# Attention and a gated MLP on one core: new planner numbers, and one more head pair in split form

## The chip, the cores and the metric

The kernel runs on one core of a Trainium2 chip. The metric is the device time of one execution in microseconds (us). Three runs of the kernel before gave 720.61, 721.33 and 721.49 us; the median is 721.33. A further execution was taken with the hardware profiler: it lasted 721.01 us, with a span from the first to the last instruction of 719.0 us.

## The reference, cut to what matters

```python
batch, n_heads, seq, head_dim = (4, 12, 448, 64)
n_tokens, d_model, d_ff = (1792, 768, 1536)

scores = scale * np.matmul(q, k.transpose(0, 1, 3, 2))
scores = np.where(mask, -1000000000.0, scores)          # causal
scores = scores - np.max(scores, axis=-1, keepdims=True)
attn = np.exp(scores)
attn = attn / (np.sum(attn, axis=-1, keepdims=True) + 1e-09)
x = np.matmul(attn, v)                                   # heads side by side: 1792 x 768

g = x @ w_gate
silu = g * (1.0 / (1.0 + np.exp(-g)))
val = x @ w_val
out = silu * val @ w_out
```

## The kernel before, in words

The four batches are four chunks of 448 tokens. A chunk has 12 attention units (one head each; unit u belongs to chunk u // 12, and units go in six pairs), and then a gated MLP (called M for the first two products, MO for the last) of 36 weight tiles: 24 for gate and value, 12 for the output.

Attention of a unit, in the names that the profile shows: the scores S on TensorE (PE, line 434); the row maximum with the mask on VectorE (DVE, line 456); the exponential p with its sums on ScalarE (ACT, line 465); the reciprocal rec on DVE (lines 476 and 477); the scaling of p by rec, one instruction for each of four row blocks, on ACT (line 486), GpSimd (POOL, line 490) or DVE (line 494); ten transposes T on PE (line 515); the copy of T to ph out of PSUM on ACT (line 286) or DVE (line 289); the product O with V on PE; the copy of O into xs.

A pair is computed in one of two forms. In float32 form ("n" in the strings NS and NP) S and O are float32 matmuls of the raw q, k and v (tiles kraw, qraw, vraw; O on line 584). In split form ("s") every operand is first parted into a high and a low part in float32r (QS, KS, VS, ph with pl), and three products of the parts are added (S from KS and QS; O on lines 554 and 556). The parting is one copy (lines 286, 289, 292 for ACT, DVE, POOL) and one subtraction (lines 308 and 311 for DVE and POOL). `nat` reads a string with the index of the pair modulo its length, so 'ns' in batch 1 makes pairs 0, 2 and 4 float32. Batch 0 is all float32, batches 2 and 3 all split.

The MLP always uses the split form: three matmuls of 448 columns (lines 691 to 693) for each 128 x 128 block of weights, 2592 in all. For chunk 0 each of the 36 weight tiles is loaded as 64-bit words (wide), scaled in place, and unpacked on DVE in three steps (wraw: lines 664, 668 and 672), and then parted into whl (one copy, one subtraction); the parted tile is stored to DRAM and loaded from there in the later chunks. whl has five buffers. The input xs is parted into xh and xl, the gated product t into hh and hl.

The order of all instructions comes from a planner that runs when the kernel is built (class Planner, `run`): it walks through time, and for each engine takes the ready operation that starts first within DELTA of the earliest, the least due time first. Where an operation can run on several engines, `finish` gives it to the one on which its modelled end plus BIAS is least. The due times come from LEN (the length given to each of five stages), FRAC, FRAC0, SLOPE and SLOPE0 (attention), XD (parting of xs), WLEAD (weights) and BOOST (reading out of M). The instructions are then issued in the planned order, and each engine works through its own list in that order, waiting where an input is late.

Of the kernel before, what the change touches and what calls it, by code (L numbers as in the profile page):

```python
# [18 lines left out]
WID = [0, 64, 192, 320, 448]  # L19
CHUNKS = [[(0, 0, 448)], [(1, 0, 448)], [(2, 0, 448)], [(3, 0, 448)]]  # L20
NR = 8
SLOPE0 = 1.0
WLEAD = 1.2
XD = [-10.0, 3.0]
CS = 0.0
UW = 0
NS = ['n', 'ns', 's', 's']
NP = ['n', 'ns', 's', 's']
LEN = [46.6, 112.0, 258.9, 133.6, 58.1]
FRAC = 0.96  # L30
FRAC0 = 0.6
SLOPE = 1.0
BOOST = 6
DELTA = {'PE': 0, 'DVE': 0.1, 'ACT': 0.1, 'POOL': 0.4, 'SP': 0.0}
BIAS = {'DVE': 1.3, 'ACT': 0.8, 'POOL': 0.8}
PVLATE = 0
LAT = {"PE": 0.29, "DVE": 0.2, "ACT": 0.23, "POOL": 0.2, "SP": 0.1}
TURN = {'ms': 0.19, 'sm': 0.19, 'mt': 0.09, 'tm': 0.085, 'ts': 0.19, 'st': 0.19, 'mv': 0.15, 'vm': 0.15, 'tv': 0.15, 'vt': 0.15, 'sv': 0.15, 'vs': 0.15}
# [12 lines left out]
def nat(flags, b, h):  # L51
    f = flags[b]
    return f[(h // 2) % len(f)] == "n"
# [32 lines left out]
class Planner:  # L86
# [9 lines left out]
    def run(self, caps):  # L96
# [6 lines left out]
        def begin(o, e, t):  # L103
            if e == "POOL":
                return max(t, lock["DVE"])
            if e == "DVE" and o.port:
                return max(t, lock["POOL"])
            return t
# [14 lines left out]
        def ready(o, e):  # L123
            t = 0.0
            for d in o.deps:
                x = d.end if d in o.soft else d.end + d.extra + (LAT[d.eng] if d.eng != e else (0.0 if e == "PE" else 0.13))
                if x > t:
                    t = x
            for i, r in enumerate(o.alloc):
                h = slots(r.tag)[sum(x.tag == r.tag for x in o.alloc[:i])]  # L130
                if h is not None:
                    if h.left:
                        return None
                    if h.end > t:
                        t = h.end
            return t

        def finish(o, e, s):
            best = s + o.alts[e][0] + BIAS.get(e, 0.0)
            for f in o.alts:  # L140
                if f != e:
                    r = ready(o, f)
                    if r is not None and begin(o, f, max(r, free[f])) + o.alts[f][0] + BIAS.get(f, 0.0) + 1e-6 < best:
                        return False
            return True

        def choose(e):
# [9 lines left out]
            if not cand:  # L157
                return None
            lim = max(min(s for s, _ in cand), free[e]) + DELTA[e]
            if e == "PE" and kind == "t":  # L160
# [52 lines left out]
def raw(t):  # L213
    return t.bitcast(F32)
# [3 lines left out]
def kernel(  # L218
# [54 lines left out]
    def op(alts, due, deps=(), alloc=(), uses=(), extra=0.0):  # L273
        first = [heads[r.tag] for r in alloc if r.tag in heads]
        o = pl_.op(alts, due, list(deps) + first, alloc, uses, extra)
        o.soft = first
        o.port = bool(alts.pop("port", False))
        o.kb = alts.pop("kb", 0)
        o.kind = alts.pop("kind", "m")
        for r in alloc:  # L280
            heads[r.tag] = o
        return o

    def copies(kind, n, out, in_, scale=1.0, engines="ADP"):
        def act():
            nc.scalar.activation(out(), in_(), AF.Copy, scale=scale)  # L286

        def dve():
            nc.vector.tensor_scalar(out(), in_(), scale, None, ALU.mult)

        def gps():
            nc.gpsimd.tensor_scalar(out(), in_(), scale, 1.0, ALU.mult, ALU.mult)

        r = {}
        if "A" in engines:
            r["ACT"] = (cost("ACT", kind, n), act)
        if "D" in engines:
            r["DVE"] = (cost("DVE", "one" if kind == "sbuf" else "two", n), dve)
        if kind == "sbuf":
            r["port"] = True  # L300
        if "P" in engines and kind == "sbuf":
            r["POOL"] = (cost("POOL", "one", n), gps)
        return r
# [9 lines left out]

    start = [sum(LEN[:i]) for i in range(len(LEN))]
    class Unit:
        def __init__(self, c, b, h, qa, qb, col):
# [5 lines left out]
            self.n = qb - qa  # L322
            self.ns, self.np = nat(NS, b, h), nat(NP, b, h)

# [30 lines left out]
    def attention(u):  # L355
# [5 lines left out]
        frac = U.w0 / done_w[c]  # L361
        base = LEN[0] * FRAC0 * frac if c == 0 else start[c] + FRAC * LEN[c] * frac
        due = lambda stage: base + (SLOPE if c else SLOPE0) * stage
        if h % 2 == 0:
# [232 lines left out]
    def split_x(c, k):  # L597
        n = TC[c]
        rh, rl = Res(f"xh{k}"), Res(f"xl{k}")
        due = start[c + 1] + XD[1 if c else 0] + 0.2 * k  # L600
        rx = xs_res[c, k]
# [11 lines left out]
    def weights(i):  # L613
        c, g = seq[i]
        due = start[c + 1] + LEN[c + 1] * g / NW
        w = wt[i] = {}
# [6 lines left out]
        def split(ra, rw):  # L623
            def newh():
                newhl()
                return w["h"]
            h = op(copies("sbuf", WC, newh, lambda: w["raw"]), due - 6 * WLEAD, [ra], [rhl], [rw])
            l = op(binary(WC, lambda: w["l"], lambda: w["raw"], lambda: raw(w["h"])), due - 5 * WLEAD, [h], [], [rw, rhl])
            wops[i] = (h, l, rhl, rhl)
            return h, l  # L630

        def keep(dst, src, deps, use, kb):
            return op({"SP": (0.3, lambda: nc.sync.dma_start(dst, src())), "kb": kb}, due - 3 * WLEAD, deps, [], [use])

        if c and (g, "hl") in stored:
            def load():
                newhl()
                nc.sync.dma_start(raw(w["hl"]), scratch[g])
            ld = op({"SP": (0.3, load), "kb": 768}, due - 10 * WLEAD, [stored[g, "hl"]], [rhl])
            wops[i] = (ld, ld, rhl, rhl)  # L640
            return
        if c:
            rw = Res("wraw")

            def load():
                w["raw"] = buf([P, WC], F32, "wraw", "wraw", f"wraw{i}")
                nc.sync.dma_start(w["raw"], scratch1[g])
            ld = op({"SP": (0.3, load), "kb": 384}, due - 12 * WLEAD, [stored[g, "raw"]], [rw])
            h, l = split(ld, rw)
# [5 lines left out]
        def load():  # L655
            w["wide"] = buf([P, WC, 2], U32, "wide", "wide", f"wide{i}")
            nc.sync.dma_start(w["wide"], wP[g].bitcast(U32).rearrange("p (n w) -> p n w", w=2))
        ld = op({"SP": (0.3, load), "kb": 768}, due - 16 * WLEAD, alloc=[r64])
        hi = lambda: w["wide"][:, :, 1]
# [35 lines left out]
    def moe(c):  # L695
        base = c * NW
        at = lambda g: start[c + 1] + LEN[c + 1] * g / NW
        prev = None
# [3 lines left out]
        for f in range(NF):  # L702
            rt = Res("t")
            tops = {}
            for w in range(2):
# [14 lines left out]
                if w == 0:  # L720
# [4 lines left out]
                    def gated(f=f):  # L725
                        t = ps[c, f, "t"]
                        nc.vector.scalar_tensor_tensor(t, t, 1.0, ps[c, f, 0][:, :N], ALU.add, ALU.mult)  # L727
                    t1 = op({"ACT": (cost("ACT", "tanh", N), tanh)}, at(gi + 1) - BOOST, [prev], [rt], [rM])
                    t2 = op({"DVE": (cost("DVE", "two", N), gated)}, at(gi + 1) - BOOST, [t1], [], [rM, rt])
                else:  # L730
                    def hprod(f=f):
                        t = ps[c, f, "t"]
                        nc.vector.tensor_tensor(t, t, ps[c, f, 1][:, :N], ALU.mult)  # L733
                    t3 = op({"DVE": (cost("DVE", "two", N), hprod)}, at(gi + 1) - BOOST, [prev, t2], [], [rM, rt])
            rhh, rhl = Res(f"hh{f}"), Res(f"hl{f}")
# [4 lines left out]
        for m in range(KD):  # L740
# [17 lines left out]
            def newo(m=m):  # L758
                ps[c, "s", m] = buf([P, T], F32, "osb", "osb", f"osb{c}_{m}")[:, :N]
                return ps[c, "s", m]  # L760
            e = op(copies("psum", N, newo, lambda m=m: ps[c, "o", m][:, :N], 0.5, engines="AD"),
                   at(gi + 1) - BOOST, [prev], [ro], [rM])

# [65 lines left out]
```

## Time and profile before

| | |
|---|---|
| median of 3 runs | 721.33 us (720.61 to 721.49) |
| profiled execution | 721.01 us |
| its span | 719.0 us |
| PE busy | 707.0 us, 98% |
| DVE busy | 378.2 us, 53% |
| ACT busy | 358.2 us, 50% |
| POOL busy | 163.3 us, 23% |
| granted TensorE clock | full speed in every slice |

The busy times are unions of intervals; PE's ends are modelled, so that its work is better read from the distance between two starts. The shares are means over stages that differ: attention of batch 0 alone (to about 61 us), the first MLP with the weight unpacking and attention of batch 1 (to about 236 us), two MLPs with attention of batches 2 and 3 (to about 580 us), the last MLP alone.

### The profile page before, as it was taken

What the parts mean: (1) busy time and instruction counts of PE and PEld (TensorE: products, weight loads), DVE (VectorE), ACT (ScalarE), POOL (GpSimd) and SP (SyncE); (2) the same over time, 40 slices, a digit from 0 to 9 for tenths busy, and PEclk for the clock granted to TensorE, in tenths of its full rate; (3) what the DMA queues carried; (4) which work ended last, traced back from release to release, by engine and by line L of the source; (5) the groups of instructions that cost most, each with busy time, mean ns of one, the idle gap of its engine ahead of it and who ended that gap; (6) DMA issues with size and microseconds to landing.
All of it is one profiled execution on the core that took longest, in us unless ns stands there. A gap on an engine that the chain in (4) does not pass through costs nothing.

```text
span 719.0 us, 10894 instructions
## 1 busy us (share of the span) xinstructions
PE 707.0 (98%) x3930; PEld 604.9 (84%) x3930; DVE 378.2 (53%) x905; ACT 358.2 (50%) x907; POOL 163.3 (23%) x212
## 2 busy tenths in 40 slices
PE   7989999999999999999999999999999999999997
PEld 4547897888888888888898988988888999999997
DVE  4779989999996435535523155455462312222100
ACT  6999685877774535525625255364473411111000
POOL 3655052154222212222412022121130000000000
PEclk9999999999999999999999999999999999999999
DMA  8568888987996855556466765544545576566671
GB/s 303 185 241 299 324 303 307 340 330 268 346 414 254 302 191 181 193 191 204 150 230 205 230 210 178 190 149 159 176 159 184 193 229 210 212 212 219 226 248 38
DMA packets 39797, 165.07 MB, mean 230 GB/s; under 512 B 4416, under 2 KB 13632, under 8 KB 39744
## 3 DMA queue, kind: packets, MB, share of 16 engines
q1 hardware_dynamic: 39744, 164.38, 65.2%
q8 instruction: 31, 0.51, 0.3%
q14 instruction: 22, 0.18, 0.1%
HBM read 130.55 MB, written 33.82 MB: 229 GB/s over the span
## 4 chain that ended last, share of the span: by engine, by line
PE 88%; ACT 6%; DVE 3%; POOL 1%; issue 1%; DMA 0%; SPq 0%; POOLq 0%; ACTq 0%
PE M L691 16%; PE M L692 16%; PE M L693 16%; PE MO L691 8%; PE MO L693 8%; PE MO L692 8%; PE T L515 6%; PE S L434 5%; ACT p L465 2%; PE O L554 2%; PE O L556 2%; ACT p L486 2%; ACT ph L286 1%; PE O L584 1%; POOL p L490 1%
## 5 line engine op out<-in xcount | busy, mean ns | idle before, releaser
L691 PE MATMUL M<-xh,whl 128*128 128x448 f32 x576 | 216.9, 377 | 0.0
L693 PE MATMUL M<-xh,whl 128*128 128x448 f32 x576 | 210.8, 366 | 0.0
L692 PE MATMUL M<-xl,whl 128*128 128x448 f32 x576 | 210.6, 366 | 0.2 <-DVE xl L308 0.2
L691 PEld LDWEIGHTS M<-xh,whl 128*128 128x128 f32 x576 | 108.3, 188 | 10.4 <-issue 0.7
L693 PEld LDWEIGHTS M<-xh,whl 128*128 128x128 f32 x576 | 108.2, 188 | 9.1
L692 PEld LDWEIGHTS M<-xl,whl 128*128 128x128 f32 x576 | 108.4, 188 | 8.6 <-DVE xl L308 0.5
L465 ACT ACTIVATE p<-p,m 64x64 f32<-64x64 f32 (+3 forms) x192 | 95.8, 503 | 38.4 <-DVE m L456 37.1
L691 PE MATMUL MO<-hh,whl 128*128 128x448 f32 x288 | 107.9, 375 | 0.0
L693 PE MATMUL MO<-hh,whl 128*128 128x448 f32 x288 | 105.4, 366 | 0.0
L692 PE MATMUL MO<-hl,whl 128*128 128x448 f32 x288 | 105.2, 365 | 0.0
L456 DVE CUSTOM_DVE_ANT_0 p<-S,mask 64x64 f32<-64x64 f32 (+1 forms) x192 | 70.5, 414 | 51.7 <-PE S L434 49.8
L286 ACT ACTIVATE ph<-T 64x448 fp32r<-64x448 f32 (+1 forms) x144 | 63.3, 498 | 38.1 <-PE T L515 37.9
L515 PE MATMUL T<-ident,p 128*128 128x128 f32 (+2 forms) x480 | 66.6, 273 | 2.9 <-ACT ph L286 2.6
L515 PEld LDWEIGHTS T<-ident,p 128*128 128x128 f32 (+2 forms) x480 | 49.5, 128 | 22.4 <-issue 9.3
L286 ACT ACTIVATE hh<-t 128x448 fp32r<-128x448 f32 x42 | 24.2, 576 | 81.3 <-DVE t L733 81.3
L727 DVE SCALAR_TENSOR_TENSOR t<-t,M 128x448 f32<-128x448 f32 x48 | 29.6, 617 | 59.5 <-ACT t L723 59.3
L691 PEld LDWEIGHTS MO<-hh,whl 128*128 128x128 f32 x288 | 54.1, 188 | 5.0 <-issue 0.4
L693 PEld LDWEIGHTS MO<-hh,whl 128*128 128x128 f32 x288 | 54.1, 188 | 4.6
L692 PEld LDWEIGHTS MO<-hl,whl 128*128 128x128 f32 x288 | 54.2, 188 | 4.1
L733 DVE TENSOR_TENSOR t<-t,M 128x448 f32<-128x448 f32 x48 | 29.6, 617 | 51.8 <-PE M L693 51.7
L486 ACT ACTIVATE p<-p,rec 128x448 f32<-128x448 f32 (+3 forms) x125 | 54.5, 500 | 3.2 <-DVE rec L477 2.2
L723 ACT ACTIVATE t<-M 128x448 f32<-128x448 f32 x48 | 26.0, 541 | 59.2 <-PE M L693 58.2
(58 smaller groups left out, 813.6 us busy)
## 6 DMA issues: line engine op xcount, KB each, us to landing
whl<-ws SPq DMA_DIRECT2D x108, 768.0 KB, 4.3
wide<-in_w_dram SPq DMA_DIRECT2D x36, 768.0 KB, 6.0
ws<-whl SPq DMA_DIRECT2D x36, 768.0 KB, 5.3
vraw<-in_v_dram SPq DMA_DIRECT2D x24, 256.0 KB, 4.4
qraw<-in_q_dram SPq DMA_DIRECT2D x24, 224.0 KB, 4.9
kraw<-in_k_dram SPq DMA_DIRECT2D x24, 224.0 KB, 4.9
out_dram<-osb SPq DMA_DIRECT2D x24, 224.0 KB, 4.7
```

Of the source, the lines that this page charges most:

```text
L286: nc.scalar.activation(out(), in_(), AF.Copy, scale=scale)
L434: nc.tensor.matmul(st[u + y][f"S{i}"][: q1_ - q0], Q[:, q0:q1_], K[:, :q1_], start=z == 0, stop=z == len(passes) - 1)
L456: nc.vector.tensor_tensor_reduce(p[:r], s[f"S{i}"][:r], mask[:r, maskX - q0 : maskX - q0 + q1_], -0.125, 3.0e38, ALU.add, ALU.min, m[:r],)
L465: nc.scalar.activation(p[:r], p[:r], AF.Exp, bias=s[f"m{i}"][:r], scale=-1.0, accum_out=sums[u % NR][:r, i : i + 1],)
L486: nc.scalar.activation(p[:r], p[:r], AF.Copy, scale=rec[u % NR][:r, i : i + 1])
L515: nc.tensor.transpose(pt[:kn, o_ + q0 - bs : o_ + q1_ - bs], s[f"p{i}"][:r, U.kb[j][0] : U.kb[j][1]], ident[:r, :r])
L691: nc.tensor.matmul(out[:, :n], a[:, w], xhi, start=first, stop=False)
L692: nc.tensor.matmul(out[:, :n], a[:, w], xlo, start=False, stop=False)
L693: nc.tensor.matmul(out[:, :n], l[:, w], xhi, start=False, stop=last)
L723: nc.scalar.activation(t, ps[c, f, 0][:, :N], AF.Tanh, scale=0.5)
L727: nc.vector.scalar_tensor_tensor(t, t, 1.0, ps[c, f, 0][:, :N], ALU.add, ALU.mult)
L733: nc.vector.tensor_tensor(t, t, ps[c, f, 1][:, :N], ALU.mult)
```

## The change

The planner's numbers are changed, BIAS and DELTA of POOL among them, and the strings of batch 1: 'nsnsss' makes pairs 0 and 2 float32 and pairs 1, 3, 4, 5 split. Pair 4 (units 20 and 21) goes from float32 to split form. Nothing else in the code changes; what changes with the numbers is the order on each engine and the engine that an operation is given to.

```diff
-SLOPE0 = 1.0
-WLEAD = 1.2
-XD = [-10.0, 3.0]
+SLOPE0 = 1.601
+WLEAD = 1.349
+XD = [-9.2, 12.1]
...
-NS = ['n', 'ns', 's', 's']
+NS = ['nnnnnn', 'nsnsss', 'ssssss', 'ssssss']
...
-DELTA = {'PE': 0, 'DVE': 0.1, 'ACT': 0.1, 'POOL': 0.4, 'SP': 0.0}
-BIAS = {'DVE': 1.3, 'ACT': 0.8, 'POOL': 0.8}
+DELTA = {'PE': 0, 'DVE': 0.12, 'ACT': 0.11, 'POOL': 0, 'SP': 0.0}
+BIAS = {'DVE': 0.84, 'ACT': 0.8, 'POOL': 0.77}
```

NP changes as NS does; LEN, FRAC, FRAC0, SLOPE and BOOST get other values.

By instructions: POOL has 119 in place of 217, ACT 646 in place of 717, DVE 1093 in place of 907. The scaling of p stands 17 times on POOL (67 before), 99 times on ACT (125) and 76 times on DVE (0). DVE also takes 31 of the copies hh, 13 of ph, 20 of VS, 10 of xh, and 19 subtractions VS; before it had none of these.

First place: POOL near the end of attention of batch 0. A name such as p10_1 is row block 1 of unit 10. Before:

```order
L490 TENSOR_SCALAR p9_3_697<-p9_3_697,rec1_77 128x448
L292 TENSOR_SCALAR xh3_93<-xs3_87 128x448
L490 TENSOR_SCALAR p10_0_753<-p10_0_753,rec2_78 64x64
L490 TENSOR_SCALAR p10_1_788<-p10_1_788,rec2_78 128x192
L490 TENSOR_SCALAR p10_2_800<-p10_2_800,rec2_78 128x320
L292 TENSOR_SCALAR KS14_910<-kraw14_668 128x448
L490 TENSOR_SCALAR p11_0_807<-p11_0_807,rec3_79 64x64
L490 TENSOR_SCALAR p11_1_813<-p11_1_813,rec3_79 128x192
L292 TENSOR_SCALAR xh4_94<-xs4_88 128x448
```

The same place on POOL now:

```order
L490 TENSOR_SCALAR p8_0_648<-p8_0_648,rec0_76 64x64
L292 TENSOR_SCALAR KS14_775<-kraw14_675 128x448
L311 TENSOR_TENSOR QS14_738<-qraw14_669,QS14_738 128x448
L292 TENSOR_SCALAR wide5_740<-wide5_740 128x768
L311 TENSOR_TENSOR KS14_775<-kraw14_675,KS14_775 128x448
L490 TENSOR_SCALAR p10_3_777<-p10_3_777,rec2_78 128x448
L292 TENSOR_SCALAR whl3_951<-wraw3_716 128x768
```

Of the scaling of units 9 to 11 one instruction is left on POOL.

Second place: DVE from the reciprocal of unit 11 (rec3) on. Before:

```order
L476 TENSOR_SCALAR rec3_79<-sums3_71 128x4
L477 RECIPROCAL rec3_79<-rec3_79 128x4
L672 SCALAR_TENSOR_TENSOR wraw3_837<-wide3_495,wraw3_837 128x768
L668 SCALAR_TENSOR_TENSOR wraw4_897<-wide4_649,wraw4_897 128x768
L672 SCALAR_TENSOR_TENSOR wraw4_897<-wide4_649,wraw4_897 128x768
```

The same place on DVE now:

```order
L476 TENSOR_SCALAR rec3_79<-sums3_71 128x4
L477 RECIPROCAL rec3_79<-rec3_79 128x4
L668 SCALAR_TENSOR_TENSOR wraw3_716<-wide3_498,wraw3_716 128x768
L494 TENSOR_SCALAR p11_2_825<-p11_2_825,rec3_79 128x320
L494 TENSOR_SCALAR p11_3_847<-p11_3_847,rec3_79 128x448
L672 SCALAR_TENSOR_TENSOR wraw3_716<-wide3_498,wraw3_716 128x768
L664 TENSOR_SCALAR wraw4_925<-wide4_617 128x768
L308 TENSOR_TENSOR whl2_782<-wraw2_638,whl2_782 128x768
L289 TENSOR_SCALAR ph11_1_949<-T11_1_934 128x384
```

Two scalings and one copy of unit 11 now stand on DVE between the steps of the weight tiles, and weight tile 2 is parted behind them.

Third place: PE around the product O of units 10 and 11, the last of batch 0. Before:

```order
L693 MATMUL M0_1_971<-xh0_90,whl1_657 128x448
L584 MATMUL O11_987<-ph10_0_914,vraw10_722 64x448
L584 MATMUL O11_987<-ph11_0_967,vraw10_722 64x448
L584 MATMUL O11_987<-ph10_1_917,vraw10_722 64x384
L584 MATMUL O11_987<-ph11_1_975,vraw10_722 64x384
L584 MATMUL O11_987<-ph10_2_927,vraw10_722 64x256
L584 MATMUL O11_987<-ph11_2_985,vraw10_722 64x256
L584 MATMUL O11_987<-ph10_2_927,vraw10_722 64x128
L584 MATMUL O11_987<-ph11_2_985,vraw10_722 64x128
L434 MATMUL S12_1_0_1011<-kraw12_544,qraw12_539 128x320
L434 MATMUL S13_1_0_1012<-kraw12_544,qraw12_539 128x320
```

The same place on PE now:

```order
L693 MATMUL M0_0_873<-xh1_91,whl0_529 128x448
L584 MATMUL O11_956<-ph10_0_909,vraw10_727 64x448
L584 MATMUL O11_956<-ph11_0_943,vraw10_727 64x448
L584 MATMUL O11_956<-ph10_1_916,vraw10_727 64x384
L584 MATMUL O11_956<-ph11_1_949,vraw10_727 64x384
L584 MATMUL O11_956<-ph10_2_927,vraw10_727 64x256
L584 MATMUL O11_956<-ph11_2_954,vraw10_727 64x256
L584 MATMUL O11_956<-ph10_2_927,vraw10_727 64x128
L584 MATMUL O11_956<-ph11_2_954,vraw10_727 64x128
L691 MATMUL M0_0_873<-xh2_92,whl0_529 128x448
L692 MATMUL M0_0_873<-xl2_98,whl0_529 128x448
```

Ahead of this O stood 15 matmuls of M0 and half of the scores of units 12 and 13; now there stand 6 matmuls of M0 and none of these scores. The rest comes behind it.

## Rows read from the trace of the kernel before

**Rows 1.** The page's first part, and busy time by stretches (from:to in us, then the length and busy time and count of each engine, granted clock, DMA share, GB/s).

```profile
PE 707.0 (98%) x3930; PEld 604.9 (84%) x3930; DVE 378.2 (53%) x905; ACT 358.2 (50%) x907; POOL 163.3 (23%) x212
...
4.00:61.00 57.00, 54.00 (x333) 29.66 (x335) 42.33 (x150) 53.81 (x170) 32.49 (x47) 1.00 0.71 251
61.00:180.00 119.00, 118.75 (x660) 99.75 (x657) 112.12 (x206) 88.82 (x193) 39.79 (x34) 1.00 0.86 313
...
240.00:580.00 340.00, 340.00 (x1953) 301.48 (x1952) 153.21 (x414) 159.21 (x425) 74.45 (x110) 1.00 0.56 191
```

**Rows 2.** The chain of waits of the first 70 us in order of time: start, length, whose work.

```profile
34.28 2.31 ACT p L465 x10
...
43.01 2.31 ACT p L465 x10
...
49.65 2.88 POOL p L490 x3
...
53.77 2.82 POOL p L490 x2
```

**Rows 3.** The timeline of PE at the end of attention of batch 0: start, length, what.

```profile
58.88 2.42 PE L584 MATMUL O<-ph,vraw 64*64 64x448 f32 x16
61.22 1.13 PE L434 MATMUL S<-kraw,qraw 64*128 64x320 f32 x8
```

**Rows 4.** The timeline of PE around one piece of attention each inside the MLP: the last M matmul ahead of the piece and the second one behind it. In order: half the scores of a float32 pair, O of a float32 pair, half the scores of a split pair, O of one unit of a split pair.

```profile
122.90 0.37 PE L693 MATMUL M<-xh,whl 128*128 128x448 f32 x1
...
124.58 0.37 PE L692 MATMUL M<-xl,whl 128*128 128x448 f32 x1
...
142.27 0.37 PE L693 MATMUL M<-xh,whl 128*128 128x448 f32 x1
...
145.22 0.36 PE L692 MATMUL M<-xl,whl 128*128 128x448 f32 x1
...
146.03 0.37 PE L693 MATMUL M<-xh,whl 128*128 128x448 f32 x1
...
147.59 0.36 PE L692 MATMUL M<-xl,whl 128*128 128x448 f32 x1
...
231.03 0.37 PE L693 MATMUL MO<-hh,whl 128*128 128x448 f32 x1
...
232.45 0.36 PE L692 MATMUL MO<-hl,whl 128*128 128x448 f32 x1
```

**Rows 5.** The timeline of DVE: the first eight row maxima (units 0 and 1) up to the first reciprocal, a reciprocal and what follows, and instructions of two sources and of one source that follow each other without a gap.

```profile
6.44 0.22 DVE L456 CUSTOM_DVE_ANT_0 p<-S,mask 64x64 f32<-64x64 f32 x1 [5.37 <-PE S L434]
...
8.32 0.36 DVE L456 CUSTOM_DVE_ANT_0 p<-S,mask 128x192 f32<-128x192 f32 x1 [0.43 <-PE S L434]
...
9.85 0.17 DVE L476 TENSOR_SCALAR rec<-sums 128x4 f32<-128x4 f32 x1
...
12.39 0.17 DVE L476 TENSOR_SCALAR rec<-sums 128x4 f32<-128x4 f32 x1 [0.20 <-ACT p L465]
...
12.69 0.18 DVE L456 CUSTOM_DVE_ANT_0 p<-S,mask 64x64 f32<-64x64 f32 x1
...
87.55 0.63 DVE L308 TENSOR_TENSOR hl<-t,hh 128x448 fp32r<-128x448 f32 x1
88.08 0.96 DVE L668 SCALAR_TENSOR_TENSOR wraw<-wide,wraw 128x768 uint32<-128x768 uint32 x1
88.95 0.96 DVE L308 TENSOR_TENSOR whl<-wraw,whl 128x768 fp32r<-128x768 f32 x1
...
186.57 0.55 DVE L664 TENSOR_SCALAR wraw<-wide 128x768 uint32<-128x768 uint32 x1
187.04 0.16 DVE L476 TENSOR_SCALAR rec<-sums 128x4 f32<-128x4 f32 x1
```

**Rows 6.** Groups of equal shape over the whole span: count, busy us, mean ns of one, idle time ahead.

```profile
L668 DVE SCALAR_TENSOR_TENSOR wraw<-wide,wraw 128x768 uint32<-128x768 uint32 x36 | 38.0, 1054 | 0.2
...
L308 DVE TENSOR_TENSOR whl<-wraw,whl 128x768 fp32r<-128x768 f32 x29 | 32.1, 1108 | 0.3
...
L664 DVE TENSOR_SCALAR wraw<-wide 128x768 uint32<-128x768 uint32 x36 | 24.7, 686 | 3.1 <-ACT wide L286 2.9 <-POOL wide L292 0.2
```

**Rows 7.** The timelines of DVE and PE: the subtraction that finishes weight tile 2 and the first matmul that reads that tile, and the same for tile 28 (tiles count from 0, in the order of the two engines' lists).

```profile
47.58 0.94 DVE L308 TENSOR_TENSOR whl<-wraw,whl 128x768 fp32r<-128x768 f32 x1
...
68.13 0.47 PE L691 MATMUL M<-xh,whl 128*128 128x448 f32 x1
...
192.15 1.49 DVE L308 TENSOR_TENSOR whl<-wraw,whl 128x768 fp32r<-128x768 f32 x1
...
194.55 0.37 PE L691 MATMUL MO<-hh,whl 128*128 128x448 f32 x1
```

**Rows 8.** The timeline of PE at its three longest waits behind the start: half the scores of units 20 and 21, O of unit 15, and the wait ahead of O of unit 22 with the matmul in front of it.

```profile
180.30 1.94 PE L434 MATMUL S<-kraw,qraw 64*128 64x320 f32 x8
...
117.12 0.37 PE L693 MATMUL M<-xh,whl 128*128 128x448 f32 x1
...
119.03 0.36 PE L692 MATMUL M<-xl,whl 128*128 128x448 f32 x1
...
220.70 0.37 PE L693 MATMUL MO<-hh,whl 128*128 128x448 f32 x1
222.15 0.47 PE L554 MATMUL O<-ph,VS 128*128 128x448 f32 x1 [1.09 <-DVE ph L308]
```

**Rows 9.** Waits of DVE between 61 and 180 us: who waited for whom, us in total, times, the longest.

```profile
DVE t L733 <- PE M L693: 2.4, 6, 0.6
DVE t L727 <- ACT t L723: 1.1, 2, 0.5
```

More of the change, by code (lines that the diff above doesn't have):

```diff
@@ L21 @@
 NR = 8
-SLOPE0 = 1.0
-WLEAD = 1.2
-XD = [-10.0, 3.0]
+SLOPE0 = 1.601
+WLEAD = 1.349
+XD = [-9.2, 12.1]
 CS = 0.0
 UW = 0
-NS = ['n', 'ns', 's', 's']
[L28 to L33, printed above, removed]
-DELTA = {'PE': 0, 'DVE': 0.1, 'ACT': 0.1, 'POOL': 0.4, 'SP': 0.0}
-BIAS = {'DVE': 1.3, 'ACT': 0.8, 'POOL': 0.8}
+NS = ['nnnnnn', 'nsnsss', 'ssssss', 'ssssss']
+NP = ['nnnnnn', 'nsnsss', 'ssssss', 'ssssss']
+LEN = [54.7, 108.3, 279.6, 129.5, 71.8]
+FRAC = 0.932
+FRAC0 = 0.749
+SLOPE = 1.027
+BOOST = 10.561
+DELTA = {'PE': 0, 'DVE': 0.12, 'ACT': 0.11, 'POOL': 0, 'SP': 0.0}
+BIAS = {'DVE': 0.84, 'ACT': 0.8, 'POOL': 0.77}
 PVLATE = 0
```

## The prediction

> **What bounds the kernel now.** I read the busy times by stretches first, then the chain of waits, then the timelines of single engines. The stretches [rows 1] show a PE that is full from 61 to 580 us: 118.75 of 119 and 340.00 of 340. A plan can win there only by taking work from PE or by removing its few waits. The start differs: to 61 us PE is busy 54.0 of 57 and ACT 53.8, and PE's pieces are spread out. The chain [rows 2] says who sets the pace: ACT with the exponentials up to about 46 us, and after that POOL, where three scalings of p last 2.88 us and two last 2.82 us. DVE is the engine to watch. It has 42 of 57 us in the start, but 112 of 119 in the next stretch, where the weight tiles are unpacked. How close that is shows in [rows 7]: tile 2 is ready at 48.5 us (47.58 + 0.94) and first used at 68.13; tile 28 is ready at 193.64 and used at 194.55. The lead of the weights has melted from 19.6 us to 0.9.
>
> The sum is made on the profiled execution: 719.05 us of span in 721.01. The median of the runs, 721.33, lies 2.3 above that span, and I add 2.3 at the end.
>
> **Pair 4 in split form.** A piece inside the MLP costs the time from the last M matmul ahead of it to the second one behind it, less two steps of M. A step is 0.203 us: (146.03 - 145.22) / 4 [rows 4]. Half the scores in float32: 124.58 - 122.90 - 0.41 = 1.27; O in float32: 2.54; half the scores in split form: 1.15; O of one unit in split form: 1.42 - 0.41 = 1.01. So the pair falls from 2 x 1.27 + 2.54 = 5.08 to 2 x 1.15 + 2 x 1.01 = 4.32. Some float32 halves cost a little more than this one, and I take -0.9. The transposes stay. The extra work of the split form (QS, KS, VS, ph with pl) is on ACT, DVE and POOL; its cover is the full PE, and what it costs without cover is in the first rival.
>
> **The start.** ACT's list up to the last copy ph of unit 11 has 102 instructions in place of 116. At 53.8 us of work for 116 (0.46 each) that is 6.4 us less. POOL's scalings, which ended the chain, are gone. In their place DVE has more, and I add up its list to the copy ph11_1, on which O of units 10 and 11 waits. From [rows 5]: eight row maxima take 9.85 - 6.44 - 0.43 = 3.0, six times 18; twelve reciprocals at 0.30 make 3.6. Two-source instructions cost 0.53 at 448 columns and 0.87 at 768, and the one-source step on line 664 costs 0.47 at 768, so an element costs half as much over a fixed 0.07. Four whole tiles at 0.47 + 0.87 + 0.87 = 2.21, one more first step and two subtractions whl make 11.0; four xl 2.1; 17 scalings and two xh at 0.10 to 0.30 make 4.4. Thirteen copies out of PSUM have no row on DVE. Their bounds are the half rate (0.27 for 384 columns) and the two-source rate (0.47); I take the latter, since no row shows the fast rate out of PSUM, and get 6.3, or 3.6 at the other end. The sum is 45.4 against about 35 for the old list.
>
> It begins at 6.44. To it come collisions with POOL and waits. Collisions show as means above the undisturbed row [rows 6, 5]: line 664 0.69 against 0.55, line 668 1.05 against 0.95, whl 1.11 against 0.95. For the few tiles of the start I take 3; the ends are 1 (POOL has half its work) and 6 (every new instruction pays as line 664 does). For waits I take 2.2: the first units cannot be hurried; the ends are 1 and 6. So ph11_1 is done at 57.0. O takes 2.42 and ends at 61.30 now [rows 3]; a good third of it can run ahead of ph11_1, so it ends at 58.7, 2.6 earlier. But less is done by then: 9 matmuls of M (1.83) and half the scores of a pair (1.27) have moved behind it, 3.1 us. Net: +0.5, with ends at -4 (DVE 3 us shorter, waits at their least) and +4.
>
> **The waits of PE behind the start.** Three large ones [rows 8]: 1.94 against the usual 1.13 for half the scores of units 20 and 21 (0.8), 1.91 - 0.41 - 1.01 = 0.5 at unit 15, and 1.45 - 0.2 = 1.25 ahead of unit 22. Together 2.55. The first belongs to the pair that changes its form, the last to a subtraction ph on DVE that the new list places elsewhere. Other such waits must be expected with a fuller DVE: I let 1.15 come back, -1.4. The ends are -2.6 and +4.
>
> **Weights.** Nothing is added while the tiles lead PE. From its present place at 61.42 us to tile 28 DVE's old list took 132.2 us. The new one, from ph11_1 to tile 28, has one tile and one step more to unpack (3.1), four more subtractions whl (3.5), eight more scalings (1.9), three more ph and pl (1.5), four more row maxima (1.4), one xl (0.5), four other copies (1.8), and less by three hl and two reciprocals (1.9): 11.8. With every wait of DVE gone (6.9 us to 180 [rows 1], 1 after it) tile 28 is ready at 57.0 + 124.3 + 11.8 = 193.1; PE asks for it at 58.7 + 133.25 + 3.1 + 0.7 (attention that moved ahead of it) = 195.8. That holds by 2.7 us, and I price it at nothing. The loads behind it stay as many (SP's list has 278 entries in both), and they stand a little earlier; the DMA engines are at 0.86 in this stretch [rows 1], so that an earlier load has little to collide with that it does not meet now: nothing either, and a load that came late would add to the same lead.
>
> **Sum.** 719.05 - 0.9 + 0.5 - 1.4 = 717.25; plus 2.3 is 719.5 us.
>
> **Rivals.** First, DVE becomes the bound of the weights, and the kernel gets slower. The place is tile 28 in the middle of MO0. If DVE keeps its 7.9 us of waits, the tile is ready at 201.0, PE stands for 5.2 us, and the time is 724.7. It decides from 2.7 us of waits on. For it: the lead of 0.9 us in [rows 7], and a list that grows by 11.8 us. Against it: the waits in [rows 9] are for results of PE and ACT, and an engine that runs late finds its inputs ready, as ACT shows, which is busy without a break in the start.
>
> Second, the start gets as short as ACT's list: 61.3 - 6.4 = 54.9 for the end of O, net -3.3 in place of +0.5, and 715.7 us. For it: DVE's 6 to 7 us of waits there, which could hide the new work; against it, DVE's own sum.
>
> Third, the collisions grow instead of shrinking. The row shows that line 664, of one source, pays 0.14 on the mean. Nineteen new instructions of that kind in the start (2.6) and about ten up to tile 28 (1.5) would make 723.6. Against it: POOL loses nearly half of its instructions, and with them the chances to collide. The Trainium skill ("GPSIMD Engine Reference", Key points) says that POOL shares its SBUF interfaces with the VectorE instructions that use two ports or have two SBUF inputs; by that rule the scalings and copies that move to DVE are of the exposed kind, while the row maxima out of PSUM are not, and the rule speaks for this rival. The rows of lines 664 and 668 agree with it.
>
> Fourth, the order changes and the time does not: gains and losses cancel at 721.3.
>
> **How the numbers follow.** The forecast has 0.42, with a range of its own from 717.5 to 721; the DVE rival 0.27, the short start 0.18, the collisions 0.08, no change 0.05. About 0.2% (1.4 us) is what a measurement of this kernel can tell from no change. Faster: 0.27 of the forecast and the short start, 0.45. Same: 0.15 of the forecast, 0.07 of the two slow rivals, and the fourth, 0.27. Slower: 0.28. The range from 715.0 to 724.5 takes in the short start and nearly all of the DVE rival, and leaves 0.2 outside.
>
> **What would show it.** In the new trace: O of units 10 and 11 ends near 58.7 us (the second rival: 55; the third: 61 or later); DVE's busy share in the start rises to over 50 of 57 and that of ACT falls to about 47; POOL's scalings leave the chain of waits; the visit of pair 4 costs 4.3 us; tile 28 is ready before PE asks for it, and PE's busy time from 180 to 240 us is not lower than now. A scaling of 448 columns on line 494 starts its follower after 0.30 us. The prediction is wrong if PE shows waits for whl between 170 and 210 us, or if line 494 runs at the two-source rate, 0.53.

## The result, and the profile after

The changed kernel takes 727.79 us (median of 6 runs, 727.51 to 730.42), the kernel before 721.22 beside it: a ratio of 1.0098, with a 95% interval from 1.0087 to 1.011. It is slower by about 1%, and above the range. The profiled execution took 727.51 us, its span 725.5, against 721.01 and 719.0: 6.5 us more.

The first part of the page, and the busy time by the stretches of [rows 1] (from:to, length, busy time and count of PE, PEld, DVE, ACT, POOL, granted clock, DMA share, GB/s), with 180 to 240 us beside them:

```profile
PE 706.6 (97%) x3936; PEld 607.8 (84%) x3936; DVE 439.4 (61%) x1091; ACT 326.4 (45%) x836; POOL 115.1 (16%) x114
...
4.00:61.00 57.00, 49.84 (x320) 28.98 (x321) 52.12 (x175) 47.88 (x152) 23.55 (x26) 0.97 0.64 222
61.00:180.00 119.00, 115.88 (x631) 95.75 (x630) 113.25 (x213) 84.40 (x187) 42.57 (x28) 1.00 0.89 318
180.00:240.00 60.00, 59.34 (x338) 51.79 (x337) 58.06 (x112) 41.57 (x94) 11.79 (x11) 1.00 0.94 347
240.00:580.00 340.00, 339.71 (x1956) 301.01 (x1955) 186.94 (x535) 139.78 (x383) 35.58 (x43) 1.00 0.56 188
```

PE has 4.2 us less to 61 us and 2.9 less to 180 us than in [rows 1]; behind 240 us next to nothing is lost. DVE is full: 52 of 57, 113 of 119, 58 of 60. In the start the granted clock is below 1.00.

Busy time hides slow work, so I use a second measure: PE's lag, the time less the undisturbed steps of all matmuls started by then (0.203 us for M and MO, 0.128 for a transpose, 0.095 and 0.145 for scores and O of the split form, 0.159 for both in float32, all read from starts of PE's timeline). It is worked out from the traces, in us:

```
at us               40    55   100   140   180   240   400
before             9.5  11.1  11.2  12.4  12.6  14.8  15.5
changed           10.0  13.9  14.1  16.9  20.1  21.8  23.0
5 wide4            9.9  14.2  14.1  16.9  18.8  19.6  20.8
9 light DVE        9.1  14.2  16.0  16.7  17.6  17.2  18.3
2 choice           9.2  10.6  14.5  15.9  19.0  19.8  20.4
13 choice, wide4   9.2  13.9  15.7  17.1  19.4  23.5  23.7
4 due times        9.5  10.2  12.2  17.7  18.9  20.6  21.0
12 due, wide4      9.8  11.3  12.6  16.5  17.1  18.0  18.3
8 old start       10.5  12.0  14.3  19.1  21.1  23.2  24.5
10 POOL moved     10.0  11.8  13.7  17.1  19.2  20.2  21.5
```

(The lower rows are experiments, by their numbers. Each row is one execution, the profiled one: that of experiment 2 is 1.8 us faster than its median, those of 13 and 9 are 1.3 and 3.0 us slower than theirs.) The changed kernel's lag grows by 2.8 us more than that of the kernel before by 55 us, then by 4.6 more between 100 and 180, and hardly more after that, 7.5 us at 400. Less the 0.8 us of matmul work that pair 4 saves, that is 6.7, close to the 6.5 of the span.

**The start.** PE's timeline at the place that loses most, and at the end of O of units 10 and 11, as in [rows 3]:

```profile
49.11 2.55 PE L515 MATMUL T<-ident,p 64*64 64x64 f32 x10 [1.96 <-DVE rec L476]
...
51.84 0.57 PE L692 MATMUL M<-xl,whl 128*128 128x448 f32 x1
52.21 0.57 PE L693 MATMUL M<-xh,whl 128*128 128x448 f32 x1
...
58.28 2.42 PE L584 MATMUL O<-ph,vraw 64*64 64x448 f32 x16
60.63 0.47 PE L691 MATMUL M<-xh,whl 128*128 128x448 f32 x1
```

PE stands 1.96 us for DVE, and behind that two M matmuls start 0.37 apart in place of 0.20. The profile puts the wait down to a reciprocal's row sum (line 476), which ended last. But these transposes, of unit 9 by the order of PE's list, do not read that reciprocal, which is unit 10's; they need one of the three buffers T, and the copy ph of unit 8, the instruction just ahead of the row sum on DVE, frees it at 48.97 us. The stretches of 2 us show why the matmuls are slow:

```profile
48.00:50.00 2.00, 0.89 (x5) 0.61 (x6) 1.97 (x8) 1.48 (x8) 0.54 (x1) 0.89 0.40 131
50.00:52.00 2.00, 1.89 (x8) 1.45 (x8) 1.40 (x5) 2.00 (x6) 0.10 (x1) 0.50 0.00 0
52.00:54.00 2.00, 2.00 (x13) 1.23 (x11) 1.97 (x6) 0.92 (x4) 0.00 (x0) 0.76 0.00 0
```

Behind the stand the granted clock is 0.50 of 2.4 GHz, which is the lower level of 1.2, and 0.76, a mean of the two levels: over these six us it costs 2 x (0.11 + 0.50 + 0.24) = 1.7. Why DVE is late shows in its timeline, with POOL's beside it: an undisturbed scaling of 448 columns with its follower, three scalings of 192 to 448 columns, a row sum of four columns, and the copy that frees the T.

```profile
31.66 0.44 DVE L494 TENSOR_SCALAR p<-p,rec 128x448 f32<-128x448 f32 x1
32.02 0.55 DVE L289 TENSOR_SCALAR ph<-T 128x384 f32<-128x384 f32 x1
...
41.18 2.55 DVE L494 TENSOR_SCALAR p<-p,rec 128x192 f32<-128x192 f32 x3
...
45.18 0.89 DVE L476 TENSOR_SCALAR rec<-sums 128x4 f32<-128x4 f32 x1
...
48.36 0.61 DVE L289 TENSOR_SCALAR ph<-T 64x448 f32<-64x448 f32 x1
```

```profile
41.30 0.56 POOL L292 TENSOR_SCALAR KS<-kraw 128x448 fp32r<-128x448 f32 x1
41.83 1.13 POOL L311 TENSOR_TENSOR QS<-qraw,QS 128x448 fp32r<-128x448 f32 x1
...
44.55 1.50 POOL L292 TENSOR_SCALAR wide<-wide 128x768 f32<-128x768 f32 x1 [1.59 <-DMA wide<-in_w_dram]
46.00 1.15 POOL L311 TENSOR_TENSOR KS<-kraw,KS 128x448 fp32r<-128x448 f32 x1
```

Alone a scaling of 448 columns lets its follower start after 0.36 us; beside POOL three take 2.55. Only the first of the three is stretched: one by one they last 1.89, 0.38 and 0.44 us in the trace, and the first ends at 43.07, 0.1 us behind POOL's subtraction. The row sum, 0.17 in [rows 5], takes 0.89 and ends at 46.07, with POOL's one-source scaling of wide (44.55 + 1.50).

**Behind the start.** Waits between 61 and 245 us (who for whom, us in total, times, longest), first of the kernel before, then of the changed one:

```profile
ACT wide L286 <- DMA wide<-in_w_dram: 7.6, 6, 2.0
...
PEld O L554 <- DVE ph L308: 1.5, 1, 1.5
...
PEld T L515 <- ACT p L486: 1.0, 3, 0.3
...
PEld S L434 <- DVE m L456: 0.5, 1, 0.5
```

```profile
ACT wide L286 <- DMA wide<-in_w_dram: 21.4, 14, 3.6
...
PEld T L515 <- ACT p L486: 3.3, 9, 0.7
PEld O L554 <- DVE ph L308: 2.7, 4, 1.1
PEld S L434 <- DVE m L456: 2.1, 4, 1.0
```

ACT stands 21.4 us at the first step of a weight tile, because the tile's load has not landed, and its list goes on in order: scalings of p that PE needs stand behind it. The chain of waits shows one such case from DVE's last step on an earlier weight tile through the load to PE (the 0.78 us of issue are ACT's step on wide itself):

```profile
196.75 0.88 DVE wraw L672
...
197.70 7.08 DMA wide<-in_w_dram
204.83 0.78 issue
205.61 1.70 ACT p L486 x4
207.36 0.95 PE T L515 x7
```

Of the 7.08 us ACT stands 0.99, and PE 0.26 for p behind it; the cases are many and each is short.

Last, tile 28 as in [rows 7], the subtraction that finishes it and the first matmul that reads it, and half the scores of pair 4 in its new form as in [rows 4]:

```profile
200.93 0.95 DVE L308 TENSOR_TENSOR whl<-wraw,whl 128x768 fp32r<-128x768 f32 x1
```

```profile
187.39 0.37 PE L693 MATMUL MO<-hh,whl 128*128 128x448 f32 x1
...
188.94 0.36 PE L692 MATMUL MO<-hl,whl 128*128 128x448 f32 x1
...
202.80 0.36 PE L691 MATMUL MO<-hh,whl 128*128 128x448 f32 x1
```

### The profile page after: what moved, and what is told of

The parts are those of the page before. It is cut to its first block, busy times and chain, and to the rows that moved or that the text cites. A ratio compares the mean times of both kernels' runs of the same rounds, so it can differ in the third digit from the quotient of the medians.

```text
span 725.5 us, 10862 instructions
## 1 busy us (share of the span) xinstructions
PE 706.6 (97%) x3936; PEld 607.8 (84%) x3936; DVE 439.4 (61%) x1091; ACT 326.4 (45%) x836; POOL 115.1 (16%) x114
## 4 chain that ended last, share of the span: by engine, by line
PE 72%; DVE 14%; ACT 6%; DMA 5%; issue 2%; POOL 0%; SPq 0%; ACTq 0%; DVEq 0%
PE M L691 13%; PE M L693 12%; PE M L692 12%; PE MO L691 8%; PE MO L693 7%; PE MO L692 7%; PE T L515 5%; DMA wide<-in_w_dram 5%; PE S L434 4%; ACT p L465 3%; DVE wraw L672 3%; PE O L554 2%; DVE wraw L668 2%; DVE p L456 2%; PE O L556 2%
## 5 line engine op out<-in xcount | busy, mean ns | idle before, releaser
L286 ACT ACTIVATE ph<-T 128x384 fp32r<-128x384 f32 (+2 forms) x131 | 57.2, 496 | 46.3 <-PE T L515 45.3
L515 PE MATMUL T<-ident,p 128*128 128x128 f32 (+2 forms) x480 | 68.2, 275 | 8.5 <-ACT ph L286 4.8
L286 ACT ACTIVATE osb<-MO 128x448 f32<-128x448 f32 x23 | 12.5, 545 | 85.7 <-PE MO L693 85.7
L486 ACT ACTIVATE p<-p,rec 64x64 f32<-64x64 f32 (+3 forms) x99 | 42.3, 478 | 11.9 <-DVE rec L477 11.3
```

Of the source, the lines that this page charges most:

```text
L486: nc.scalar.activation(p[:r], p[:r], AF.Copy, scale=rec[u % NR][:r, i : i + 1])
L515: nc.tensor.transpose(pt[:kn, o_ + q0 - bs : o_ + q1_ - bs], s[f"p{i}"][:r, U.kb[j][0] : U.kb[j][1]], ident[:r, :r])
```

## The experiments

Theories: **A**, DVE, full with the scalings and copies it was given, delivers late whatever attention needs of it. **B**, the new lengths and due times put work in a worse order. **C**, the split pair costs more than it saves. **D**, formed after the first four runs: ACT stands in its list for loads that the ring of three buffers wide lets start too late. **E**: a collision with POOL makes the stand at 47 us, and the stand the clock's fall. Medians follow, with the ratio to the kernel before and its 95% interval.

**The parts of the change.** Each part alone, or taken back alone.

Experiment 1, the changed kernel with the old choice of engine:

```diff
-DELTA = {'PE': 0, 'DVE': 0.12, 'ACT': 0.11, 'POOL': 0, 'SP': 0.0}
-BIAS = {'DVE': 0.84, 'ACT': 0.8, 'POOL': 0.77}
+DELTA = {'PE': 0, 'DVE': 0.1, 'ACT': 0.1, 'POOL': 0.4, 'SP': 0.0}
+BIAS = {'DVE': 1.3, 'ACT': 0.8, 'POOL': 0.8}
```

> The changed kernel with the two tables that choose the engine (DELTA, BIAS) as they were before; due times, lengths and the split pair stay as changed. DVE's list falls from about 1,100 to 913 instructions, POOL's rises to 223. Theory A (DVE saturated by the scalings and copies it was given makes attention's results late): the loss goes, 718 to 721 us, DVE busy under 49 of 57 us in the start, waits of PE behind the start at most 4 us. Rival B (the new due times and lengths move work in the wrong order): still 725 to 728. Rival C (the split pair costs more than its matmuls save): still above 724, with the waits of PE around pair 4.

733.29 us (1.0149, 1.0114 to 1.0184): slower still. PE's waits between 61 and 245 us have two new long ones:

```profile
PE MO L693 <- DVE whl L308: 3.1, 1, 3.1
PE M L691 <- DVE t L727: 2.9, 1, 2.9
```

None of the theories had this. The due times with the old choice make another plan, with stands of its own.

Experiment 2, the reverse: the kernel before with the two new tables (the same diff with its signs changed).

> The kernel before with the changed DELTA and BIAS alone: DVE's list grows from 907 to 1,097 instructions, POOL's falls from 217 to 119, ACT's from 717 to 625. Theory A: slower, 725 to 730 us (the changed kernel's loss, plus the 0.8 us that pair 4 saves there). Rival B: 720 to 722. Rival C: 720 to 722.

727.29 us (1.0086, 1.0056 to 1.0116), as A said.

Experiment 3, the kernel before with the split pair alone:

```diff
-NS = ['n', 'ns', 's', 's']
-NP = ['n', 'ns', 's', 's']
+NS = ['nnnnnn', 'nsnsss', 'ssssss', 'ssssss']
+NP = ['nnnnnn', 'nsnsss', 'ssssss', 'ssssss']
```

> The kernel before with the changed NS and NP alone: pair 4 in split form, 22 matmuls more for PE, 5 instructions more for DVE, 6 each for ACT and POOL. Theory A: pair 4's visits fall from 5.1 to about 4.3 us and the time by 0.5 to 0.9, 720.3 to 720.8 us. Rival C: 722 or more, since the split form's copies come late.

724.20 us (1.0045, 1.0028 to 1.0061). A missed it; C has the size, but not the reason. PE's waits, and the stretch behind the stand that ends at 219.44 us:

```profile
PE MO L693 <- DVE whl L308: 2.8, 1, 2.8
```

```profile
220.00:222.00 2.00, 2.00 (x8) 1.22 (x7) 1.85 (x4) 1.58 (x4) 0.00 (x0) 0.50 0.94 390
```

With six more instructions each for ACT and POOL and five for DVE weight tile 32 comes late; PE stands for it, and the clock falls.

Experiment 4, the kernel before with the new due times alone:

```diff
-SLOPE0 = 1.0
-WLEAD = 1.2
-XD = [-10.0, 3.0]
+SLOPE0 = 1.601
+WLEAD = 1.349
+XD = [-9.2, 12.1]
...
-LEN = [46.6, 112.0, 258.9, 133.6, 58.1]
-FRAC = 0.96
-FRAC0 = 0.6
-SLOPE = 1.0
-BOOST = 6
+LEN = [54.7, 108.3, 279.6, 129.5, 71.8]
+FRAC = 0.932
+FRAC0 = 0.749
+SLOPE = 1.027
+BOOST = 10.561
```

> The kernel before with the changed lengths, slopes, leads and offsets alone (LEN, FRAC, FRAC0, SLOPE, SLOPE0, WLEAD, XD, BOOST): as many instructions per engine as before, in another order. Theory A: within 2 us of before, 719 to 723. Rival B: 725 to 728, the whole loss.

727.01 us (1.0082, 1.0067 to 1.0097): B. So the parts cost 6.2, 3.1 and 5.9 us alone, 15.2 added up, and 6.6 together. They do not add: each of two parts costs nearly the whole loss alone. What two of them share is ACT's wait for loads of wide, here between 61 and 245 us in experiment 2 and then in 4:

```profile
ACT wide L286 <- DMA wide<-in_w_dram: 20.1, 14, 2.9
```

```profile
ACT wide L286 <- DMA wide<-in_w_dram: 19.1, 14, 3.2
```

**A fourth buffer, lists untouched.** The planner goes on planning with three buffers wide, so every list stays word for word; one buffer osb less pays for it.

```diff
+BUFS = {'wide': 4, 'osb': 1}
...
-        return pool.tile(shape, dt, tag=tag, name=name, bufs=CAPS[base])
+        return pool.tile(shape, dt, tag=tag, name=name, bufs=BUFS.get(base, CAPS[base]))
```

Experiment 5, in the changed kernel:

> The changed kernel with four buffers for the packed weights (wide) in place of three, paid for by one buffer osb less; every engine's list stays the same, word for word. A load of wide can then start one tile earlier. Theory D (ACT stands in its own order at the step on wide whose load has not landed, 21.4 us from 61 to 245 us against 7.6 before, and p and ph behind it come late): that row falls below 10 us, the waits of PE for p L486 with it, and the time falls to 722 to 724.5 us. Theory A (DVE's list is too long, whoever waits for what): ACT's row falls as well, but DVE stays at 56 to 58 of 60 us and the time at 726 or more.

724.05 us (1.0044, 1.0029 to 1.0059), 3.7 less than the changed kernel's 727.79. ACT's row, and the second stretch:

```profile
ACT wide L286 <- DMA wide<-in_w_dram: 6.4, 6, 2.5
```

```profile
61.00:180.00 119.00, 117.56 (x640) 96.88 (x641) 116.73 (x217) 85.97 (x188) 39.95 (x29) 1.00 0.89 327
```

PE's wait for p (line 486) falls from 3.3 to 0.9 us with it. D holds for a good half of the loss. DVE stays full.

Experiment 6, the same in the kernel before:

> The kernel before with the same four buffers wide and one osb, all lists the same. It is the control for what the smaller osb costs and for what the earlier loads give a plan whose ACT stands only 7.6 us for them. Theory D: within 0.2% of before, 719.5 to 722.5 us. If the earlier loads collide with other transfers, or one osb holds up the outputs, slower than 722.5.

721.06 us (0.9996, 0.9986 to 1.0005): no change. The smaller osb costs nothing, and the fourth buffer gives nothing to this plan. ACT's row is 9.5 us here, so a row of that length need not cost anything.

Experiment 7, the same in the kernel of experiment 3:

> The kernel before with the split pair 4 (the third experiment) and four buffers wide. There PE stood 2.8 us for the weight tile 32, at the end of a chain of DVE's weight steps, a store of whl (3.94 us) and loads of wide (6 us). If the three buffers make that chain: the wait at tile 32 goes, the spread of the runs closes, and the pair's saving of 0.8 us is left, 720.0 to 721.0 us. If the store of whl or DVE makes it: 723 to 725 as in the third experiment.

722.05 us (1.0009, 0.9999 to 1.0018): a miss, between the two. Of the stand of 2.8 us for tile 32, 2.1 are left; the ring was a small part of it. The time fell by 2.1 us all the same, though ACT's row was short in experiment 3 (7.9 us); by the lag, 1.2 us of it came before 180 us.

Experiments 12 and 13 put the fourth buffer into the kernels of 4 and 2, and tell the ring from DVE:

> The fourth experiment's kernel (before, with the new due times alone, 727.0 us) with four buffers wide and one osb, all lists the same. There ACT stood 19.1 us for loads of wide between 61 and 245 us, and PE 1.6 us for a row maximum of DVE at 127 us, behind which the clock fell. Theory D (the ring is the common cause): ACT's row falls below 10 us and the time to 721.5 to 724. If the due times lose by their order alone: 726 or more, whatever ACT's row does.

> The second experiment's kernel (before, with the new choice of engine alone, 727.3 us) with four buffers wide and one osb, all lists the same. ACT stood 20.1 us for loads of wide there. Theory D: 722 to 724.5 us. Theory A (DVE's fullness, whoever waits for the loads): 725.5 or more, as DVE's list of 1,097 instructions is untouched.

Experiment 12 took 722.55 us (1.0018, 1.0009 to 1.0028), experiment 13 took 727.68 (1.0095, 1.0061 to 1.0128). ACT's row in 12 and then in 13:

```profile
ACT wide L286 <- DMA wide<-in_w_dram: 4.2, 4, 1.6
```

```profile
ACT wide L286 <- DMA wide<-in_w_dram: 9.7, 9, 2.0
```

The row falls in both, but the time only in the first: 4.5 of 5.9 us go. The due times lose by the ring. The choice of engine does not, as far as its spread tells (724.09 to 729.78 us in five runs of experiment 2, 726.14 to 731.6 in four of 13): there D falls and A is left, but DVE was not made lighter in that plan.

**DVE lighter.** Experiment 9, the kernel of experiment 5 without the sign step:

```diff
-        d1 = op(dv("two", sign), due - 9 * WLEAD, [d0], [], [r64, rw])
+        d1 = op(dv("two", lambda: None), due - 9 * WLEAD, [d0], [], [r64, rw])
```

> The fifth experiment's kernel (changed kernel, four buffers wide) without the sign step of the weight tiles on line 668: its 36 instructions of 0.95 us are left out on DVE, some 33 us of the 230 up to the end of MO0; the weights come out without their sign. All other lists stay. It asks what is left of the loss after the fourth buffer: 2.8 us. Theory A as the rest of the cause (DVE too full, its results for attention late): DVE falls from 117 to about 98 of 119 us between 61 and 180 us, the small waits of PE there go, 720 to 721.5 us. If the order that the due times give is the rest, whatever DVE's load: 723.5 to 725.

719.87 us (0.9985, 0.9969 to 1.0002), 4.2 less than experiment 5. The stretches:

```profile
61.00:180.00 119.00, 118.70 (x667) 98.78 (x664) 98.93 (x198) 87.33 (x192) 39.26 (x29) 1.00 0.91 341
180.00:240.00 60.00, 60.00 (x349) 53.91 (x347) 48.97 (x101) 39.46 (x92) 11.54 (x10) 1.00 0.89 328
```

PE is full again with the very order of the changed plan, so the order alone is not what loses. The 4.2 us are more than the 2.8 that were left, and the kernel before was not run without the sign step: a part of the gain may be one that any plan would have. What lighter DVE alone would do, with three buffers, was not tried either. The traces show how closely the ring hangs on DVE: with three buffers a load of wide starts when DVE's last step (line 672) on the tile three before it ends, within 0.3 us for all 28 loads between 61 and 245 us in the kernel before, within 0.1 for 28 of 29 in the changed one, and with four buffers for 2 of 29 (experiment 5). So the ring's 3.7 us and DVE's share can't be priced apart by these runs.

**The start.** Experiment 8 uses the old BIAS (BIAS0) for what is planned before 55 us:

```diff
-BIAS = {'DVE': 0.84, 'ACT': 0.8, 'POOL': 0.77}
+BIAS = {'DVE': 0.84, 'ACT': 0.8, 'POOL': 0.77}; BIAS0 = {'DVE': 1.3, 'ACT': 0.8, 'POOL': 0.8}
...
-            best = s + o.alts[e][0] + BIAS.get(e, 0.0)
+            bias = BIAS0 if s < 55 else BIAS; best = s + o.alts[e][0] + bias.get(e, 0.0)
...
```

> The changed kernel with the old DELTA-free choice rule (BIAS as before) only for what is planned in the first 55 us, and the new one behind it: 16 instructions go back from DVE to POOL. It asks what the start's choice is worth. Theory A for the start (DVE sets its pace since it has the scalings): DVE's busy time from 4 to 61 us falls from 52 to below 47, no clock fall from 48 to 56 us, the end of O of units 10 and 11 near 59, and 2 to 3 us less in all, 724.5 to 726. If the loss of the start comes from the due times: no change, 727 to 729.

728.77 us (1.0104, 1.0087 to 1.0121). The stretches:

```profile
4.00:61.00 57.00, 54.13 (x326) 30.01 (x328) 50.04 (x161) 53.80 (x172) 27.19 (x37) 1.00 0.76 267
61.00:180.00 119.00, 113.58 (x622) 93.69 (x624) 110.55 (x204) 79.78 (x172) 35.84 (x30) 1.00 0.83 296
```

A miss: PE gets most of its start back (lag 12.0 at 55 us, 13.9 in the changed kernel), with no fall of the clock, and loses more behind it (19.1 at 140 us, 16.9 in the changed kernel). All four executions had a mean clock of 0.999 or 1.000 and took 728.06 to 728.94 us: a loss of this size needs no fall of the clock.

Experiment 10 moves two instructions of POOL:

```diff
-    order = pl_.run(CAPS)
+    order = pl_.run(CAPS); late = [o for o in order if o.idx in (750, 752)]; order = [o for o in order if o not in late]; k = [o.idx for o in order].index(653) + 1; order[k:k] = late
```

> The changed kernel with two subtractions of POOL (the low halves of QS and KS of units 14 and 15, 1.13 and 1.15 us, from 41.8 and 46.0 us) moved behind POOL's scaling at 49.5 us; nothing else moves. In the changed kernel three scalings of DVE on line 494 lasted 2.55 us beside the first and a row sum (line 476) 0.89 us in front of the second, then PE stood 1.96 us for the reciprocals, and its clock was granted at 0.50 and 0.76 from 50 to 54 us. Theory E (the collision makes the stand, and the stand the clock's fall): L494 falls to about 1.2 us for the three, the stand to 0.5 or less, the clock stays at 1.00, and the time falls by 2.5 to 3 us, 724.5 to 725.5. If DVE's list alone makes the stand: it stays above 1.4 us, and the time within 1 us of 727.8.

726.67 us (1.0083, 1.0066 to 1.01), 1.1 less than the changed kernel; the two intervals overlap. DVE's timeline at the two places, and PE's:

```profile
41.15 1.44 DVE L494 TENSOR_SCALAR p<-p,rec 128x192 f32<-128x192 f32 x3
...
44.59 0.15 DVE L476 TENSOR_SCALAR rec<-sums 128x4 f32<-128x4 f32 x1
```

```profile
39.41 1.02 PE L515 MATMUL T<-ident,p 64*64 64x64 f32 x7 [2.00 <-ACT ph L286]
```

E's first half holds: 2.55 falls to 1.44, 0.89 to 0.15, and the stand at 47 us is gone. Its price does not: the lag at 55 us is 2.1 us less (11.8), at 400 us 1.5. In the profiled execution PE stood 2.00 us ten us earlier (1.42 in the changed kernel) and the clock fell there. Another execution took 726.74 us at a mean clock of 1.000, so the clock's fall is not most of the loss. The rule of the Trainium skill ("GPSIMD Engine Reference", Key points) that POOL shares its SBUF interfaces with VectorE instructions that use two ports or have two SBUF inputs agrees with these rows.

Experiment 11 prices a stand by itself: the kernel before with two subtractions of 0.53 us ahead of the subtraction ph of unit 22, on which PE stands in [rows 8].

```diff
+    junk = cpool.tile([P, maskX + P], F32, tag="junk", name="junk")
+
+    def more():
+        nc.vector.tensor_tensor(junk, mask, mask, ALU.subtract)
...
+            if u == 22 and stk:
+                lo.alts["DVE"] = (lo.alts["DVE"][0], lambda f=lo.alts["DVE"][1]: (more(), more(), f()))
```

> The kernel before with two extra subtractions on DVE (0.53 us each, into a tile that nobody reads) ahead of the subtraction ph of unit 22, for which PE already stands 1.09 us at 221 us. It measures the price of a longer stand by itself. If a stand costs its own length: 1.06 us more, 722.2 us. If the clock falls behind the longer stand as it did in the other runs (0.50 to 0.77 for 4 us, some 1.7 us): 723.5 to 724.2 us, and a clock below 1.00 behind 223 us.

722.79 us (1.0024, 1.0013 to 1.0035). PE's timeline (its line numbers are 7 higher) and the stretch behind it in the profiled execution:

```profile
224.02 0.48 PE L561 MATMUL O<-ph,VS 128*128 128x448 f32 x1 [1.86 <-DVE ph L308]
```

```profile
224.00:226.00 2.00, 1.98 (x7) 1.84 (x8) 2.00 (x4) 0.00 (x0) 0.00 (x0) 0.63 0.20 76
```

This execution took 724.41 us at a mean clock of 0.998. Five of the seven had 1.000 and took 722.24 to 723.41, 1.2 us above the kernel before at their median. So the two subtractions cost about their 1.06 us in most executions, and the clock's part comes only in some.

Experiment 14, the kernel of experiment 7 with a planner that knows of the fourth buffer:

```diff
-    order = pl_.run(CAPS)
+    order = pl_.run({**CAPS, **BUFS})
```

> The kernel before with the split pair 4 and four buffers wide that the planner knows of too, so that its lists change (DVE 917, ACT 725, POOL 216 instructions). If the stand at tile 32 in the third and seventh experiments came from a plan made for three buffers: no stand above 1 us, 720.0 to 721.0 us. If any new order costs, as all of them did so far: 722 to 727.

728.98 us (1.0105, 1.0088 to 1.0122): a miss, dearer than either range. Its longest wait of PE is of a kind already met in experiment 1:

```profile
PE M L691 <- DVE t L727: 1.9, 1, 1.9
```

No version here beats the kernel before by more than a measurement can tell, not even experiment 9, which leaves work out.

## Why the prediction was wrong

- **Pair 4, -0.9: right as PE's work.** Half its scores in split form cost 188.94 - 187.39 - 0.41 = 1.14 (forecast 1.15), and the matmul work falls by 0.8. The extra work on the other engines, which I let the full PE cover, was not free where it could be seen alone: the pair made the kernel before 3.1 us slower (experiment 3).
- **The start, +0.5: measured about +2.8.** Right were the move of load (ACT 47.88, forecast about 47; DVE 52.12, forecast over 50) and POOL's leaving the chain. O of units 10 and 11 ended at 60.6, not 58.7. Two steps failed. One is the work of DVE: ph11_1 was done at 58.1, 1.1 us late. I had put 3 us of collisions on it, with the reason that POOL has half its work, and read them from the steps of the weight tiles. Those paid nothing (11.0 us forecast and measured, from start to start); the 17 scalings and two xh took 7.6 for 4.4, and the reciprocals with their row sums 5.5 for 3.6, since 12 row sums had a mean of 0.37 where [rows 5] show 0.17. A part of that is the size: 0.36 for 448 columns, not 0.30. Shorter row maxima (16.6 for 18.0) gave 1.4 back, and the waits were 2.2 as forecast. The other step is the path: I let a third of O run ahead of ph11_1 on a PE that is there in time. PE stood 1.96 us at 47 us and ran at half the clock behind it; from then on its timeline has no wait, and it came to O only at 58.28. That stand and the clock's fall were in no term. It was the third rival's mechanism; experiment 10 gives 2.1 us of the start back without that stand, but only about 1 us of the time, which is not clear of noise.
- **PE's waits behind the start, -1.4: measured +4.6 to 180 us.** This is the step that decided. I looked at three long waits and let 1.15 us come back, with +4 as the worst end. What came were many short ones, for p, ph and row maxima, and their source had two parts: ACT standing for loads of wide (experiments 5 and 12) and a full DVE (experiments 2, 9 and 13; 9 has no control in the kernel before). I had priced a full DVE by the weights alone.
- **Weights, 0: right in price, wrong in working.** Tile 28 was ready at 200.93 + 0.95 = 201.9, 8.8 us later than forecast, and used at 202.8. The lead is 0.9 as before, since PE was late by as much, and that is luck. PE did not wait for whl, and line 494 did not run at 0.53: neither of the two signs of being wrong that I had named came.
- **The loads of weights, 0: wrong.** I argued that earlier places in SP's list and a DMA share of 0.86 leave nothing to pay, and that a late load would add to the tile's lead. It pays elsewhere: ACT's list goes on in order, and its waits for loads, 21.4 us in place of 7.6, stand ahead of p.
- **The first rival** had the engine right and the place wrong: a full DVE did not stop PE at tile 28, but spread over attention. With -0.9, +2.8 and +4.6 the sum on the span is 725.55, against 725.5; as the last two are read from a lag that counts every matmul, this must come out and confirms no cause.

## What to carry to other kernels

Do not price an engine at 95% only by the deadline of its bulk work: ask what else stands in its list, and what an in-order engine holds back when it stands at a step whose load has not landed. One more buffer with untouched lists is a cheap test for that, and the length of the row of waits does not replace it: it gave 3.7 and 4.5 us in two plans with a row of 19 to 21 us and nothing in a third (experiment 13), 2.1 us with a row of 7.9 (experiment 7) and nothing with one of 7.6. Parts of a retuned plan can't be priced one by one: alone they cost 15.2 us here, together 6.6.

## What the hardware showed that I had not expected

- Scalings of DVE on line 494 beside POOL's two-source step stretch from 1.44 to 2.55 us for three, nearly all of it on the first, and a row sum of four columns beside a one-source step of POOL from 0.15 to 0.89, although POOL has half as many instructions as before. A few instructions pay, by a us or more, and the means hide it: 14 of the 17 scalings up to 61 us were undisturbed.
- A stand of PE can be followed by some 4 us at 0.50 to 0.77 of the full clock (1.96 us in the changed kernel, 2.78 in experiment 3, 1.86 in experiment 11), and the same kernel shows it in some executions and not in others. The times spread with it: three executions of experiment 9 at a mean clock of 0.993 took 722.00 to 722.88 us, the seven at 0.994 to 1.000 took 717.83 to 721.30. The kernel before had 0.998 or more in all its executions.
